# Holding DMA transposes behind weight blocks, a second split of the early v projection, and new orders for five engines

## The chip, the core and the metric

The kernel runs on one core of a Trainium2 chip. Its engines work side by side, each through its own list of instructions in order: TensorE (PE, matmuls, with weight loads shown apart as PEld), ScalarE (ACT), VectorE (DVE), GpSimd (POOL) and SyncE (SP), which here issues nearly all DMAs. They wait for each other by semaphores. The metric is the device time of one execution in microseconds (us).

## What is computed

Two mixers of tokens share one input and are blended by a gate for each row:

```python
x = A_x                                            # 2048 x 448, bf16
g = sigmoid((x * gate_w).sum(-1, keepdims=True))
a = attention(x, wq, wk, wv, wo, beta)             # 16 heads of 28, 4 segments of 512 rows
b = token_mlp(x, w1, b1, w2, b2)
return g * a + (1 - g) * b

# attention, for each segment s and head, phi(t) = t + 1 if t > 0 else exp(t)
p     = softmax(q_s @ k_s.T * 28**-0.5 + causal_mask)
a_mem = (phi(q_s) @ M) / (phi(q_s) @ z + 1e-6)
o     = sigmoid(beta) * a_mem + (1 - sigmoid(beta)) * (p @ v_s)
M, z  = M + phi(k_s).T @ v_s, z + phi(k_s).sum(rows)
# then o @ wo

# token_mlp mixes along the 2048 rows
u = gelu(layernorm(x).T @ w1 + b1)                 # 448 x 1792
y = (u @ w2 + b2).T                                # 2048 x 448
```

## The kernel before

**Pieces and names.** The 2048 rows are 16 tiles of 128, or 4 chunks of 512, one for each segment. The name of an operation is a short word with its numbers:

- `warm`, `fill`: matmuls on constants that keep TensorE running until data arrive. `trx`: TensorE transposes of chunk 0 of x, which `xTcp` copies from PSUM.
- `k0a` to `k0d`, `q0a`, ... and `v03a`, `v67a`, ...: projections (line 705). They use half of the array's rows at a time, two halves side by side, so matmuls come in pairs. `cpk`, `cpq`, `cpv` and `gt` evacuate their PSUM banks (lines 741, 753, 800, 824, 827). `padk`, `padx` and `padq` copy the loaded wk and wq into the padded layout of the heads (line 649).
- `sc4_0` ... are score groups: unit pair 4 (a unit is four heads of one segment, 16 units in all), fill 0 of 5 (line 967). A group fills PSUM banks 0 to 3; `exp4_0` on ScalarE (line 976) empties them, and only then can the next group start. `mask` on GpSimd zeroes what is above the diagonal. `pv` (line 1005) multiplies by v, `mem` reads the memory, `mst` (line 852) adds a segment to it, `wo` is the output projection and `ag` its gated copy (line 1061).
- `ek`, `mk`, `phk`: phi of a key chunk (lines 785, 787, 789), into one of two buffers; `tk1_3` (line 792) is the DMA transpose of chunk 1, head group 3, from this buffer, and frees it. `eq`, `mq`, `phq` are the same for queries.
- `u0-0` to `u13-15` and `y0-0` to `y15-13`: matmuls of the MLP, 14 tiles of u with 16 steps each, 16 tiles of y with 14 steps (line 278; line 280 where one is cut into four matmuls of 32 columns that run side by side). `gsq`, `gvh`, `garg`, `gth`, `gelu` are the gelu (lines 1081, 1084 or 1087, 1089, 1092, 1094); `fin` is the last blend (line 1112). `bns`, `bna`, `ln` are the layernorm (lines 910, 912, 924).
- On SyncE's list: `ldx`, `ldwv`, `ldwk`, `ldwq`, `ldwo` load inputs. `ldw1_0` to `ldw1_6` and `ldw2_0` to `ldw2_7` load blocks of W1 and W2 (lines 570, 576), 1 MB and 0.9 MB, for two tiles of u or of y each. They share three slots, so the fourth block waits until the two tiles of the first are computed. `dtx1_0` ... are DMA transposes of chunks 1 to 3 of x (line 529), each in a piece of three column blocks (_0) and of one (_1). `gk`, `gq` gather the tail dimensions of heads through DRAM (lines 766, 771). `out` stores the result (line 1116).

**What sets the order.** Every engine's sequence is written out by hand in the table `ORDER`, together with the PSUM bank or buffer that an operation takes. `plan` (line 154) reads it, gives every operation its engine (some may go to ScalarE or VectorE) and adds the waits for buffers. An operation's `deps` become semaphore waits ahead of it on its own engine. A waiting instruction holds everything behind it on that engine, and on SyncE that means every later DMA.

**Early v tiles.** `project` (line 698) makes two pairs of outputs from four tiles. For each pair it emits a first part (a or b) and a rest (c or d). With `cut` the first pair's first part is split once more: v03s needs only the first two loaded pieces of WV, v03a all three.

Of the kernel before, what the change touches and what calls it, by code (L numbers as in the profile page):

```python
# [74 lines left out]
class Sched:  # L75
# [78 lines left out]
    def plan(self, order):  # L154
# [22 lines left out]
        self.columns(seq["PE"])  # L177
        assert sum(len(v) for v in seq.values()) == len(self.ops)
# [5 lines left out]
        while moved:  # L184
            moved = False
            for e in ENGINES:
                while head[e] < len(seq[e]):
                    o = seq[e][head[e]]
# [107 lines left out]
def pool_cost(n):  # L296
# [7 lines left out]
        warm fill0 fill1 fill2 fill3 fill4 trx0_1=4 trx0_0=5 trx1_1=6 fill5 gtr trx1_0=7 v03s v03a v03b v03c k0a=45  # L304
        v03d k0c k0b=67 q0a k0d q0b q0d q0c v67a=45 sc0_0 k1a=76 v67c k1c sc0_1 k1b=54 k1d sc0_2 q1a=76 q1b=54 sc0_3
        q1c q1d pv0=7 sc0_4 u0-0:3=6 u1-0=7 btr=5 u2-0=4 u1-1:2 u2-1 u0-3 u1-3 u2-2 u3-0=5 u0-4:2 sc1_0 u0-6 u2-3
        u1-4:2 u0-7 u2-4 u3-1 u0-8 u3-2 u1-6 u3-3 u1-7:3 u2-5 u0-9 u2-6 u3-4 sc1_1 u0-10:2 u1-10:2 u3-5 u0-12 u1-12
        u2-7 u3-6 u1-13 u0-13 u2-8 u0-14:2 u3-7 u1-14:2 u3-8 sc1_2 u2-9:3 pv1=6 u2-12 u3-9:2 u5-0:2=7 u2-13 sc1_3
        u3-11 u2-14 u4-0=6 u5-2 u2-15 u4-1:2 u3-12 u4-3 u5-3 u4-4 u3-13:3 sc1_4 u4-5 u5-4:4 u7-0:2=4 u4-6 u7-2:2 u5-8
        u4-7:2 u7-4 u5-9 sc2_0 u4-9:3 u5-10 u7-5:2 u4-12:3 u6-0=5 u4-15 u5-11:2 u7-7 u6-1:2 sc2_1 u5-13:2 u7-8 u5-15  # L310
        u6-3:3 u7-9 pv2=6 u7-10 sc2_2 u6-6:2 u7-11 mst0=6 u6-8 u7-12 pv3=7 sc2_3 u6-9 u7-13 u6-10 u7-14 u6-11:3 u7-15
        u6-14:2 u9-0=6 u8-0:2=7 sc2_4 u9-1:2 u8-2:2 u9-3 u8-4:2 mem4=4 u8-6:6 u9-4:2 u8-12 sc3_0 u9-6 u8-13 u9-7
        u8-14:2 u9-8:8 pv4=5 sc3_1 k2a=47 k2b=65 k2c k2d sc3_2 q2a=74 q2b=65 q2c q2d sc3_3 v96a=47 v96b=65 v96c v96d
        sc3_4 u10-0:5=7 pv5=5 mem5=6 u10-5:3 pv6=4 sc4_0 mem6=6 u11-0=5 u10-8:2 u13-0=4 u11-1 u13-1 u11-2:3 u12-0=6
        u11-5 u10-10:4 u11-6 u10-14 u11-7 u10-15 sc4_1 u13-2:2 u11-8 u12-1 u11-9:6 u12-2 u13-4 u11-15 u13-5 sc4_2
        u12-3:2 mst1=7 u13-6 u12-5 u13-7 u12-6:2 mem7=7 sc4_3 u12-8:2 u13-8:2 wo3=5 pv7=7 sc4_4 u12-10 u13-10:2
        u12-11:3 wo1=5 u13-12:2 u12-14:2 wo0~2=7 u13-14:2 wo2=5 sc5_0 k3a=76 k3b=54 k3c k3d sc5_1 v14a=76 pv8=5 v14c
        pv9=4 wo5=5 mem9=7 sc5_2 q3a=46 q3b=57 q3c q3d sc5_3 y0-0:2=4 y3-0=6 y0-2 y3-1 y1-0:2=7 y0-3 y1-2 y0-4:2
        y3-2:2 y1-3 mem8=5 y1-4 y0-6 sc5_4 y3-4 y1-5:2 y3-5:3 wo4=5 y1-7 y0-7 sc6_0 y0-8 y1-8 y0-9:3 y3-8:2 y1-9 y3-10
        y1-10:2 sc6_1 y1-12 y3-11:2 y1-13 y0-12 y3-13 y0-13 wo6=5 mem11=7 sc6_2 mst2=6 pv11=5 pv10=7 y4-0:2=4 sc6_3  # L320
        y5-0:2=5 y4-2 y5-2 y2-0:3=7 mem10=6 y2-3:2 y5-3 y4-3 sc6_4 y2-5 y4-4:2 y5-4 y2-6 y4-6 y2-7 y4-7 y2-8 y5-5
        y6-0=6 y5-6 y2-9 sc7_0 y5-7 y6-1 y4-8 y2-10 y5-8 y4-9 y6-2 y4-10 y6-3:2 y4-11:2 sc7_1 y6-5 y4-13 y5-9 y2-11
        y6-6 y5-10 y6-7 y2-12:2 y5-11:3 mem12=4 sc7_2 y6-8:2 pv12=7 wo7=4 y7-0:2=5 sc7_3 y7-2 mem13=7 y7-3 y6-10
        y7-4:5 y6-11 y7-9 wo8=4 y7-10:2 y6-12 y7-12:2 sc7_4 pv14=7 y6-13 pv13=4 wo10=5 wo11=6 wo9=4 pv15=5 y8-0=7
        mem14=6 y8-1:4 y9-0=4 y8-5 y9-1 mem15=6 y9-2 y8-6 y9-3 y8-7 y9-4:2 y8-8 y9-6 y11-0:2=6 y8-9:2 y11-2:2 y9-7
        y11-4 y10-0=5 y9-8 y10-1 y9-9:2 y10-2:2 y8-11:2 y9-11 y11-5 y8-13 y9-12 y11-6 y9-13 y10-4:3 y11-7 y10-7:2
        y11-8 y10-9 y11-9 y10-10:4 y11-10 wo15=7 wo14=4 y11-11 wo12=5 wo13=7 y13-0:2=4 y11-12:2 y13-2 y12-0=5 y14-0=7
        y12-1:2 y14-1:4 y12-3:2 y13-3 y15-0=6 y13-4 y14-5 y15-1 y13-5 y15-2 y12-5 y14-6:2 y15-3 y14-8 y13-6:3 y14-9
        y12-6 y13-9:2 y15-4:2 y14-10 y15-6:2 y13-11 y14-11 y15-8:3 y14-12 y15-11:2 y14-13 y12-7:2 y13-12 y15-13 y13-13
        y12-9:5 y15-0~2=7 y15-1~2 y15-2~2 y15-3~2 y15-4~2 y15-5~2 y15-6~2 y15-7~2 y15-8~2 y15-9~2 y15-10~2 y15-11~2  # L330
        y15-12~2 y15-13~2
    """,
    "ACT": """
        ldx1 ldgwb ldgw xTcp0_01 xTcp0_00 xTcp0_10 cpv0 gt0 cpv2 gt1 gt3 gt2 cpk0_1 ek0_0 cpk0_3 cpq0_3 cpk0_2 cpq0_2
        cpq0_1 gt4 ek0_1 tb exp0_0=2 cpv6 gt7 gt6 exp0_1=3 cpk1_2 exp0_2=4 exp0_3=0 cpq1_1 cpv5 cpq1_2 gt5 exp0_4=1
        eq1_1 exp1_0=5 ek0_2 eq1_2 exp1_1=6 eq1_0 gsq0 gsq1 exp1_2=2 ek0_3 gth0 exp1_3=3 ek1_0 gsq2 gth1 exp1_4=0 gsq3
        ek1_1 gth2 exp2_0=1 gsq4 gth3 exp2_1=4 gsq5 eq1_3 exp2_2=5 gth4 gth5 exp2_3=6 gsq7 gsq6 exp2_4=0 gth7 gth6
        ek1_3 exp3_0=2 gsq8 gsq9 gvh9 ek1_2 exp3_1=3 cpk2_1 cpk2_3 cpq2_3 exp3_2=1 cpq2_1 cpv8 gt8 exp3_3=4 cpv10 gt10
        cpv11 gt12 gt11 gt9 exp3_4=7 ek2_1 eq2_0 exp4_0=0 gth8 gth9 eq2_1 eq2_2 gsq10 exp4_1=5 gvh10 gsq11 exp4_2=6
        gvh11 exp4_3=2 gth10 ek2_0 gth11 exp4_4=3 ag1 gsq12 eq2_3 gsq13 gvh13 exp5_0=1 ek2_3 cpk3_0 cpk3_2 cpk3_3  # L340
        exp5_1=4 cpv14 gt14 cpv15 gt15 ag5 gth12 gth13 exp5_2=7 cpq3_1 cpv13 gt13 exp5_3=0 ek2_2 eq3_1 exp5_4=5 eq3_0
        exp6_0=2 exp6_1=3 ag6 exp6_2=6 eq3_2 exp6_3=0 exp6_4=5 exp7_0=1 exp7_1=4 exp7_2=7 eq3_3 exp7_3=2 ag8 exp7_4=3
        ag10 ag11 ag9 ag15 ag14 ag13
    """,
    "DVE": """
        ob0 bns0 bns3 bna0 bna3 gw bns1 xTcp0_11 bns2 padk1 padx0 padk0 cpv1 padq0 padq3 bna1 padq2 bna2 cpv3 cpk0_0
        ln0 mk0_0 ln2 ln1 phk0_0 bns4 cpv4 bna4 cpq0_0 bns5 bns7 bna5 bns6 bna7 bns8 cpv7 mk0_1 bna6 ln3 bns13 cpk1_0
        cpk1_1 cpk1_3 cpq1_3 bns9 bns12 bns11 bns10 bna10 cpq1_0 bna12 omgh ln6 bna8 bna13 bna11 bna9 ta0 bns15 bns14
        b2c ln4 b1c ln5 ln7 bna14 bna15 ln8 gcol1 ln10 mo0 b1h b1s ln9 oc0 ln12 ln11 gh phk0_1 rec0 mk0_2 ln13 ln14
        mq1_1 ln15 mg0 gcol0 oc1 phk0_2 gvh0 gvh1 garg0 garg1 mq1_2 mo1 oc2 ta1 rec1 mq1_0 mk0_3 oc3 phk0_3 gelu0 mg1  # L350
        gvh2 phq1_0 gelu1 garg2 oa0 gvh3 mo2 garg3 mg2 gelu2 mk1_0 mo3 mk1_1 phk1_1 oa1 gvh4 gelu3 garg4 ta2 gvh5
# [33 lines left out]
def build_kernel(nc, X, WQ, WK, WV, WO, BETA, W1, B1, W2, B2, GW, OUT):  # L385
# [312 lines left out]
    def project(name, outs, prio, cut=False):  # L698
# [21 lines left out]
        for k in range(0, len(outs), 2):  # L720
            a, b = outs[k : k + 2]
            whole = run(a, 0, True), run(b, 1, True)
            if cut and k == 0:
                part(name + "s", [seq[0:2] for seq in whole], (), R_wv[0:2])
                whole = [seq[2:] for seq in whole]
# [519 lines left out]
```

## Time and profile before

| | |
|---|---|
| time, median of 3 | 175.21 us (175.08 to 175.9) |
| profiled execution | 174.94 us, of which the profile's span is 173.2 us |
| granted TensorE clock | full |
| matmuls and weight loads | 1838 and 1846 |
| DMA | 24.55 MB, 142 GB/s over the span |
| start of sc0_0, sc5_0, sc7_4 | 16.46, 98.20, 141.41 us |
| end of the last matmul | 170.79 us |
| landing of a W1 block, min, median, max | 5.8, 6.8, 12.3 us |
| landing of a W2 block | 5.1, 5.5, 8.1 us |
| landing of a tk transpose | 2.4, 2.5, 7.7 us |
| landing of a dtx transpose | 4.1, 5.1, 5.9 us |

A landing is counted from the start of the issue on SyncE. In the page's table of busy time each entry gives the time, the share of the span and the number of instructions. In the rows of 40 slices, a slice is 4.33 us and a digit is its busy share in tenths. In an answer in order of time the columns are start, length, engine, line, operation, tiles, shapes, count, and in brackets the engine's idle time before it with what ended it; "issue" is time for which the profile shows no wait. A TensorE matmul's end is modelled, so the matmul row can look busy through a wait; the weight-load row shows it better.

### The profile page before, as it was taken

To read this page: it belongs to the slowest core of one execution; us is meant where nothing else is said; L and a number is where in the kernel's file an instruction comes from. 1 tells how busy PE (TensorE), PEld (TensorE's weight loads), DVE (VectorE), ACT (ScalarE), POOL (GpSimd) and SP (SyncE) were. 2 spreads that over 40 slices of the span, in tenths; PEclk is the share of its full clock that TensorE was granted. 3 is DMA by queue.
4 is the path that set the end of the run, shared out by engine and by line. 5 is a ranking of instruction groups with operands and counts; after the bars stand their busy time and mean duration, and the time that the engine had idled before them with its cause. 6 is when DMAs were issued, how large, how long until landed. Compare 5 with 4: busy or idle time off the path is not lost.

```text
span 173.2 us, 4524 instructions
## 1 busy us (share of the span) xinstructions
PE 166.6 (96%) x1838; PEld 80.9 (47%) x1846; DVE 144.7 (84%) x323; ACT 128.5 (74%) x154; POOL 69.6 (40%) x99
## 2 busy tenths in 40 slices
PE   8999989999999899999999999999999999999994
PEld 4445334444445345445454445544544445555552
DVE  3769999949999998999989899998997989983115
ACT  2459989799999999999999999987957767004000
POOL 7030097252514620095074472536725955150000
PEclk9999999999999999999999999999999999999999
DMA  5999989248557992097835207211641597408103
GB/s 148 276 183 358 293 143 245 76 89 241 136 139 222 144 169 47 13 271 205 108 67 172 63 0 217 45 30 34 190 113 34 143 300 215 119 22 243 53 0 106
DMA packets 49749, 24.55 MB, mean 142 GB/s; under 512 B 14257, under 2 KB 49489, under 8 KB 49729
## 3 DMA queue, kind: packets, MB, share of 16 engines
q1 hardware_dynamic: 49576, 24.16, 58.0%
q8 instruction: 14, 0.23, 0.6%
q10 hardware_dynamic: 152, 0.12, 0.2%
q14 instruction: 7, 0.05, 0.1%
HBM read 18.76 MB, written 2.36 MB: 122 GB/s over the span
## 4 chain that ended last, share of the span: by engine, by line
PE 60%; DVE 27%; DMA 4%; ACT 3%; issue 2%; SPq 2%; ACTq 0%
PE t L278 35%; PE t L705 13%; PE t L280 5%; PE t L967 4%; PE t L1005 4%; DVE t L1089 3%; DVE t L1094 3%; DVE t L1087 3%; DMA t<-in_A_wk_dram 2%; DVE t L1021 2%; DMA t<-in_A_wo_dram 2%; DVE t L789 2%; DVE t L1040 2%; DVE t L910 1%; ACT t L1081 1%
## 5 line engine op out<-in xcount | busy, mean ns | idle before, releaser
L278 PE MATMUL t<-t 128*128 128x448 bf16 (+2 forms) x441 | 85.8, 347 | 1.1 <-issue 0.8
L976 ACT ACTIVATE t<-t 128x2048 bf16<-128x2048 f32 x40 | 75.0, 1876 | 8.4 <-PE t L967 8.2
L979 POOL TENSOR_SCALAR_AFFINE_SELECT t<-t 128x512 bf16<-128x512 bf16 x64 | 44.4, 717 | 53.7 <-ACT t L976 53.2
L278 PEld LDWEIGHTS t<-t 128*128 128x128 bf16 x449 | 41.5, 98 | 41.2 <-issue 5.9
L705 PE MATMUL t<-t 64*128 64x512 bf16 (+1 forms) x308 | 35.2, 367 | 0.9 <-DMA t<-in_A_wv_dram 0.3
L1036 POOL TENSOR_TENSOR t<-t 128x448 bf16<-128x448 f32 x12 | 15.2, 1274 | 23.6 <-DVE t L1034 13.3
L705 PEld LDWEIGHTS t<-t 64*128 64x128 bf16 x308 | 15.4, 94 | 17.8 <-PE t L705 1.3
L280 PE MATMUL t<-t 128*32 128x448 bf16 (+1 forms) x356 | 20.4, 355 | 0.3 <-DMA t<-in_A_wo_dram 0.3
L1112 DVE SCALAR_TENSOR_TENSOR t<-t 128x448 bf16<-128x448 f32 (+2 forms) x17 | 10.8, 648 | 11.4 <-PE t L278 11.2
L1061 ACT ACTIVATE t<-t 128x448 bf16<-128x448 f32 x10 | 7.2, 724 | 13.8 <-PE t L278 13.5
L967 PE MATMUL t<-t 28*128 28x512 bf16 (+3 forms) x256 | 15.8, 301 | 0.5
L1005 PE MATMUL t<-t 128*32 128x512 bf16 (+3 forms) x256 | 11.4, 300 | 0.5 <-DVE t L893 0.5
L280 PEld LDWEIGHTS t<-t 128*32 128x32 bf16 x356 | 8.4, 96 | 6.8 <-issue 1.8
L967 PEld LDWEIGHTS t<-t 28*128 28x128 bf16 x256 | 4.5, 92 | 14.4 <-ACT t L976 6.2
L1021 DVE STREAM_TRANSPOSE t<-t 128x512 f32<-128x512 f32 x16 | 11.0, 695 | 0.3 <-PE t L1005 0.2
L1042 DVE STREAM_TRANSPOSE t<-t 128x512 bf16<-128x512 bf16 x16 | 11.0, 692 | 0.0
L910 DVE BATCH_NORM_STATS2 t<-t 128x6 f32<-128x448 bf16 x16 | 9.4, 611 | 1.9 <-DMA t<-in_A_x_dram 1.8
L1081 ACT ACTIVATE t<-t 128x448 f32<-128x448 f32 x14 | 8.8, 635 | 1.3 <-DVE t L1094 0.7
L1005 PEld LDWEIGHTS t<-t 128*32 128x32 bf16 x256 | 6.6, 96 | 6.1 <-POOL t L979 1.5
L1089 DVE SCALAR_TENSOR_TENSOR t<-t 128x448 f32<-128x448 f32 x14 | 9.0, 657 | 0.1
L1087 DVE TENSOR_SCALAR t<-t 128x448 f32<-128x448 f32 x10 | 6.5, 667 | 3.1 <-ACT t L1081 3.1
L1019 DVE STREAM_TRANSPOSE t<-t 128x512 f32<-128x512 f32 x12 | 8.4, 700 | 0.7 <-PE t L280 0.3
(73 smaller groups left out, 165.4 us busy)
## 6 DMA issues: line engine op xcount, KB each, us to landing
t<-in_B_w_dram SPq DMA_DIRECT2D x7, 1024.0 KB, 6.8
t<-in_B_w_dram SPq DMA_DIRECT2D x8, 896.0 KB, 5.5
out_dram<-t SPq DMA_DIRECT2D x15, 112.0 KB, 1.8
t<-in_A_x_dram SPq DMA_DIRECT2D x3, 448.0 KB, 5.9
t<-in_A_wo_dram SPq DMA_DIRECT2D x4, 98.0 KB
t<-in_A_wk_dram SPq DMA_DIRECT2D x1, 336.0 KB, 4.0
t<-in_A_wq_dram SPq DMA_DIRECT2D x1, 336.0 KB, 4.6
spare_heads<-t SPq DMA_DIRECT2D x8, 32.0 KB
```

Source lines behind the costliest of these rows:

```text
L278: return e.matmul(out, w, x, skip_group_check=True, **kw)
L280: last = e.matmul(out[q : q + 32], w[:, q : q + 32], x, skip_group_check=True, **kw)
L705: last = e.matmul(bank(o["b"])[:, 0 : o["n"]], o["w"](r, c), o["x"](r, c), start=first, stop=end, skip_group_check=True)
L910: op("DVE", lambda e: e.bn_stats(st6[:, t, :], xh[:, t, :]), reads=[R_x[t]], writes=[R_st6[t]], name=f"bns{t}", cost=512, prio=P_PROJ - 10)
L967: last = e.matmul(bank(hl)[:, c0 : c0 + w], kT[r, hg, s * 512 + j * 128 : s * 512 + j * 128 + 128], qT[r, hg, s * 512 + 128 * j : s * 512 ...
L976: op("ACT", lambda e: e.activation(pslot(g), ps[:, 0:4, :], ACT.Exp, scale=SCALE), reads=R_bank[0:4], writes=[g.res], take=g, name=f"exp{p ...
L979: op("POOL", lambda e, c0=c0: e.affine_select(pslot(g)[:, :, c0 : c0 + 128], pslot(g)[:, :, c0 : c0 + 128], pattern=[[0, 4], [1, 128]], co ...
L1005: last = e.matmul(bank(cb)[32 * hl : 32 * hl + 32, 128 * j : 512], vaug[:, 4 * s + j, 32 * h : 32 * h + 32], pslot(P_fill[u // 2][f])[:, h ...
L1021: dv(lambda e: e.transpose(t2[:, 0, :], bank(cb)[:, 0:512]), [bres(cb)], [R_tt[tb][0]], "ta", 630, use=(cb,))
L1036: op("POOL", lambda e: e.tensor_tensor(o3, n3[0], n3[1], op=ALU.add), reads=R_tt[tb], writes=[R_ob[tb]], name=f"o{u}", cost=1280, port=Tru ...
L1087: alt=("DVE", lambda e: e.tensor_scalar(vh[:, q, :], bank(b)[:, 0:D], 0.5, b1h[:, ft : ft + 1], op0=ALU.mult, op1=ALU.add), dve_cost(448)))
L1089: op("DVE", lambda e: e.scalar_tensor_tensor(gg[:, q, :], gg[:, q, :], 1.0, vh[:, q, :], op0=ALU.add, op1=ALU.mult), reads=[R_gg[q], R_vh[ ...
```

## The change

Three things change together.

1. In `plan`, a DMA transpose of phi of k (`tk`) or of chunk 2 or 3 of x (`dtx2`, `dtx3`) gets one more dependency: the last operation over 1 MB that stands ahead of it on SyncE's list. These are the blocks of W1 and W2 by the sizes that the code notes for them. The transpose, and all that is behind it on the list, is then issued only when that block has landed. The purpose is that a transpose and a weight block ahead of it are not in flight together.
2. `project` with `cut` now splits the second pair's first part too: v03t (first two pieces of WV), then v03b.
3. All five orders are new. The work is the same; its place, its banks, and for some evacuations the engine differ.

The code:

```diff
         self.columns(seq["PE"])
+        big = None
+        for o in seq["SP"]:
+            if big is not None and o.name.startswith(("tk", "dtx2", "dtx3")):
+                o.deps = o.deps + [big]
+            if o.nbytes > 1e6:
+                big = o
...
-            if cut and k == 0:
-                part(name + "s", [seq[0:2] for seq in whole], (), R_wv[0:2])
+            if cut:
+                part(name + "st"[k // 2], [seq[0:2] for seq in whole], (), R_wv[0:2])
                 whole = [seq[2:] for seq in whole]
```

The orders, cut to what the prediction speaks of:

```diff
 "PE":
-        warm fill0 fill1 fill2 fill3 fill4 trx0_1=4 trx0_0=5 trx1_1=6 fill5 gtr trx1_0=7 v03s v03a v03b v03c k0a=45
-        v03d k0c k0b=67 q0a k0d q0b q0d q0c v67a=45 sc0_0 k1a=76 v67c k1c sc0_1 k1b=54 k1d sc0_2 q1a=76 q1b=54 sc0_3
-        q1c q1d pv0=7 sc0_4 u0-0:3=6 u1-0=7 btr=5 u2-0=4 u1-1:2 u2-1 u0-3 u1-3 u2-2 u3-0=5 u0-4:2 sc1_0 u0-6 u2-3
...
-        y1-10:2 sc6_1 y1-12 y3-11:2 y1-13 y0-12 y3-13 y0-13 wo6=5 mem11=7 sc6_2 mst2=6 pv11=5 pv10=7 y4-0:2=4 sc6_3
+        warm fill0 fill1 trx0_1=4 trx0_0=5 trx1_1=6 fill2 fill3 gtr fill4 trx1_0=7 fill5 v03s v03a v03t v03b v03c v03d
+        k0a=54 k0b=67 k0c k0d q0a q0b q0d q0c v67a=54 sc0_0 k1a=67 v67c k1c sc0_1 k1b=45 k1d sc0_2 q1a=76 q1b=45 q1c
+        q1d sc0_3 u1-0:2=7 u0-0:2=6 u1-2 pv0=4 u1-3 u0-2:3 sc0_4 u0-5:2 u1-4 u0-7 btr=4 u3-0=5 u1-5:3 u3-1 u0-8 u3-2
...
+        y3-11:3 y0-13 sc6_2 mem11=6 pv10=5 mst2=4 mem10=7 pv11=6 sc6_3 y5-0=5 y2-0=4 y5-1 y2-1 y5-2:2 y2-2 y5-4:2
+        y4-0=7 y5-6:2 y4-1:3 sc6_4 y4-4 y6-0=6 y5-8 y6-1 y5-9 y4-5 y2-3 y4-6 y2-4 y4-7 y5-10 y6-2 y4-8 sc7_0 y5-11
 "ACT":
-        ldx1 ldgwb ldgw xTcp0_01 xTcp0_00 xTcp0_10 cpv0 gt0 cpv2 gt1 gt3 gt2 cpk0_1 ek0_0 cpk0_3 cpq0_3 cpk0_2 cpq0_2
-        cpq0_1 gt4 ek0_1 tb exp0_0=2 cpv6 gt7 gt6 exp0_1=3 cpk1_2 exp0_2=4 exp0_3=0 cpq1_1 cpv5 cpq1_2 gt5 exp0_4=1
+        ldx1 ldgwb ldgw xTcp0_11 cpv2 gt2 cpv0 cpv1 gt1 gt3 gt0 cpk0_0 ek0_0 cpk0_2 cpk0_3 cpq0_3 cpq0_2 gt4 cpq0_1
+        ek0_1 exp0_0=2 cpv6 gt7 gt6 exp0_1=3 cpk1_3 cpk1_2 exp0_2=4 ek0_2 cpq1_0 cpq1_1 exp0_3=0 cpv5 tb gt5 exp0_4=1
 "SP":
-        ldx0 ldx2 ldwv0 ldwv1 ldwv2 ldwk0 ldwk=0 ldwq0 ldb2 ldbeta ldwq=1 dtx1_0 dtx1_1 ldx4 ldx8 ldx12 ldw1_0 ldw1_1
-        tk0_0 gk0_0 gk0_2 ldb1 ldw1_2 gk0_1 gq0_2 gq0_1 gq0_3 gq0_0 gk0_3 gq0_h1 gq0_h0 gq0_h2 gk0_h1 gk0_h0 tk0_1
-        tk0_2 ldw1_3 tk0_3 ldw1_4 ldw1_5 tk1_1 dtx3_1 dtx2_1 dtx3_0 ldwo1 dtx2_0 tk1_0 gk2_1 ldw1_6 gq2_1 gk2_0 tk1_3
-        gq2_0 ldwo2 ldw2_0 ldwo3 gk2_2 gk2_3 tk1_2 gq2_3 gq2_2 gq2_h2 tk2_1 ldwo0 gk2_h0 gk2_h1 gq2_h0 gq2_h1 ldw2_1
-        gk3_1 ldw2_2 gk3_0 gk3_2 tk2_0 gk3_3 tk2_2 gq3_2 tk2_3 out3 gq3_1 ldw2_3 gk3_h0 gq3_0 out0 gq3_3 gq3_h0 gq3_h1
+        ldx0 ldx2 ldwv0 ldwv1 ldwv2 ldwk0 ldwk=0 ldwq0 ldwq=1 ldbeta ldb2 dtx1_0 dtx1_1 ldx4 ldx12 ldb1 ldx8 dtx2_1
+        tk0_0 ldw1_0 ldw1_1 gk0_2 gk0_1 gk0_3 ldw1_2 gq0_2 gq0_1 gq0_0 gk0_0 gq0_3 gk0_h1 gk0_h0 gq0_h1 gq0_h2 gq0_h0
+        tk0_1 tk0_2 ldw1_3 ldwo2 tk0_3 ldw1_4 dtx2_0 dtx3_0 tk1_1 tk1_0 dtx3_1 ldw1_6 ldw1_5 gk2_1 ldwo1 gq2_3 ldwo3
+        tk1_3 gk2_0 ldwo0 gk2_2 tk1_2 gq2_2 gq2_0 gk2_3 tk2_1 ldw2_1 gq2_1 ldw2_0 gq2_h1 gk2_h1 gq2_h0 ldw2_2 gq2_h2
+        gk2_h0 tk2_0 tk2_3 gk3_0 gq3_3 tk2_2 gq3_0 gq3_2 gq3_1 ldw2_3 gk3_1 out3 gq3_h2 gk3_3 out0 gq3_h0 out1 gk3_2
...
```

## Prediction

> **What bounds the kernel now.** I read the page's busy table first, then its slices, then the waits of TensorE, then its order of time with the stretches between score groups, last the SyncE queue.
>
> ```profile
> PE 166.6 (96%) x1838; PEld 80.9 (47%) x1846; DVE 144.7 (84%) x323; ACT 128.5 (74%) x154; POOL 69.6 (40%) x99
> ...
> PE   8999989999999899999999999999999999999994
> ...
> DVE  3769999949999998999989899998997989983115
> ACT  2459989799999999999999999987957767004000
> ...
> L278 PE MATMUL t<-t 128*128 128x448 bf16 (+2 forms) x441 | 85.8, 347 | 1.1 <-issue 0.8
> L976 ACT ACTIVATE t<-t 128x2048 bf16<-128x2048 f32 x40 | 75.0, 1876 | 8.4 <-PE t L967 8.2
> ```
>
> TensorE is full from end to end; ScalarE and VectorE are full in the slices that hold the attention (about 12 to 120 us) and idle at the tail. So the end is set by TensorE work plus whatever makes TensorE wait, and in the attention ScalarE can be what it waits for: each of the 40 score groups needs the exp of the group before.
>
> A busy PE hides waits, so I turn to rates. From the order of time: 18 plain matmuls of 448 columns take 3.51 us (0.195 each), 14 pairs of key projections 3.13 us (0.224 a pair), 14 pairs of v 2.77 us (0.198), a score group 0.33, a PV unit 0.54 to 0.66 (I take 0.60), an mst 0.5. For ScalarE a full exp is followed 1.78 us after its start by the next instruction; a copy takes 0.5, an exp of 512 or a gelu step 0.53. With these I add up, for each stretch from one score group to the next, the work that the two orders put there. Stretch 0_1 (sc0_1 to sc0_2), for one: a group and seven pairs of k1, 0.33+1.57 = 1.9 on TensorE; exp0_1 and one copy, 1.78+0.52 = 2.3 on ScalarE; measured 2.38, so ScalarE set it.
>
> | stretches | PE work | longer of PE and ACT, stretch by stretch, summed | measured |
> |---|---|---|---|
> | before, sc0_0 to sc5_0 (25) | 77.7 | 81.4 | 81.7 |
> | before, sc5_0 to the last matmul (15) | 72.8 | 73.7 | 72.6 |
>
> The first row holds 4.0 us in which TensorE has no work (81.7-77.7); the second none. Ahead of the first score group, from 6.50 to 16.46 us, the work is 12 pairs of v, 24.5 of k and q, 7.5 more of v: 12x0.198+24.5x0.224+7.5x0.198 = 9.35 us of 9.96, so 0.6 us is lost there. The weight-load row shows by what:
>
> ```profile
> 8.49 1.76 PEld L705 LDWEIGHTS t<-t 64*128 64x128 bf16 x20 [0.55 <-DVE t L649]
> 10.66 2.93 PEld L705 LDWEIGHTS t<-t 64*128 64x128 bf16 x30 [0.41 <-DVE t L649]
> ...
> 16.43 0.13 PEld L967 LDWEIGHTS t<-t 28*128 28x128 bf16 x4 [0.49 <-DVE t L800]
> ```
>
> The padding copies of wk, then of wq (L649) are waited for, then the evacuation of q0 (L800). Two later stalls are on the matmul row itself:
>
> ```profile
> 58.91 0.92 PE L278 MATMUL t<-t 128*128 128x448 bf16 x4 [0.60 <-issue]
> ...
> 91.81 0.94 PE L280 MATMUL t<-t 128*32 128x448 bf16 x16 [0.28 <-DMA t<-in_A_wo_dram]
> ```
>
> [...] the tk transpose issued alone at 43.0 lands after 2.4 us, the one issued at 52.3 behind a weight block of 51.9 lands after 7.0, 0.6 us after that block.
>
> **The change part by part.**
>
> *The waits of tk, dtx2, dtx3.* No byte is moved less. Each waits for the last weight block ahead of it in the queue. In the new queue: tk0_0 and one dtx2 stand ahead of every block and wait for none. tk0_1 waits for w1_2, issued about 24, 7.0 to land as before: 31; the gathers ahead of it end at 34 as now, so nothing. tk0_3 waits for w1_3: issue when u0 and u1 are done, near 37, plus 5.8: 43; behind it stands w1_4, whose slot u3 frees only at 45; the next user of its buffer, the exp of k1_1, now stands behind exp2_0, near 48. dtx2_0 waits for w1_4 (issue 45.5 plus 6.1): 51.6; behind it are dtx3, tk1_1, tk1_0, five issues of 1.2 to 2.2, and landings of 4 to 6 put the last near 65 against 74 for v9-12 and 57 for xT2 against 66. tk1_3 and tk1_2 wait for w1_5, near 70, needed by mst1 near 90; behind them ldwo0, wanted by wo2 at 90. tk2_0 waits for w2_2 (97 plus 5.4), needed near 121; behind it the gathers of k3 and q3, wanted by sc7_2 near 134. Slack is 1 us at tk0_3, 3 at tk0_1 and 8 or more elsewhere: cost 0. Its possible gain: at 58.3 to 58.9 TensorE stands 0.60 us with no wait that the profile shows, while a block, a tk and two dtx are in flight (the DMA share is 1.99 in 56 to 58). Whether that is the cause the trace does not say: 0 to 0.6, I take 0.3.
>
> *The second cut of v03.* v03t needs the first two pieces of WV, but stands behind v03a, which waits for the third. Nothing can start earlier: 0.
>
> *Head of the order.* k0a goes behind v03d: 3 pairs (0.6 us) fill the 0.3 us that TensorE stands before 8.49. ldwq is issued at 4.7, not 5.64, and q0a goes behind k0d, 11 pairs later than now; so the pads of q are long done: 0.2 to 0.4. Three copies of xT go to VectorE, 0.41 each as the one there now; it stands 0.7 and 1.2 us for wk and wq anyhow. Limit of the sum 0.6; I take 0.5, so sc0_0 near 15.9.
>
> *Middle.* By the same rates the new order's longer-of-two sum from sc0_0 to sc5_0 is 81.3 against 81.4. It is 0.9 behind at sc1_0 (stretch 0_2 now has 14 projection pairs, 3.47, and ScalarE an exp and three small jobs, 3.35) but has 1.4 us more matmul work done by then, and has caught up at sc1_1. No gain. The last ldwo, at 88.4, leaves the 0.28 stall at 91.8; it moves to near 75: 0.3, partly inside a stretch that ScalarE sets, so 0.2.
>
> *Tail.* Same work, 72.8 in both, no loss to win. Nearer deadline: y6 starts 6.25 us of TensorE work after y0 ends, whose slot its block w2_3 takes; landing takes 5.5, at most 8.1 for any W2 block. 0 at the median, 0.9 at 7.0. I take 0.
>
> Sum: 0.5+0.3+0.2 = 1.0: 175.2-1.0 = **174.2**.
>
> **Rivals.** *Absorbed.* ScalarE starts exp0_0 only behind 17 copies, tanhs and exps, and VectorE is full: earlier projections then wait for evacuations instead of pads. For: the wait at 16.43 is for a VectorE copy, and the middle's sum is equal. Against: the new order takes one copy off VectorE there. Gain 0.2: **175.0**. *Late blocks, slower.* w1_0 and w1_1 now stand behind tk0_0, which needs phi of k0 (14.5): issue near 15.8 instead of 11.96. With the 9.6 that w1_0 took, it lands at 25.4, while u1-0, moved ahead of sc0_4, wants it at 25.0 (15.9, plus 8.8 for three stretches, plus 0.33): 0.4. If w2_3 takes 7.0, 0.9 more; head gain 0.2. **176.3**. Against: 9.6 was spent behind 1.3 MB of x, which now has a clear road. *All waits fall:* half of the middle's 4.0 us goes: near 172.7; nothing in the sums supports it.
>
> **Numbers.** Forecast 0.50, absorbed 0.29, late blocks 0.18, the last 0.03. The range runs from 173.2, twice the forecast's gain, to 175.9, most of the way to the late blocks. Faster by over 0.5% means under 174.33: most of the forecast's spread and the last, with a little of the absorbed: 0.50; within 0.5%: 0.32; slower 0.18.
>
> **What would show it.** Right: no wait for L649 on the weight loads of 8 to 11 us, first score group near 15.9; no stall of 0.6 by "issue" near 58; tk landings of 2.4 to 3; sc5_0 at 97.2 or so instead of 98.20. Wrong: an L278 wait for B_w near 25 or 126, SyncE waits after which a gather or a block lands late, or a first score group that is no earlier.

## The result, and the profile after

The changed kernel takes **174.22 us** (median of four runs, 174.12 to 174.29), the kernel before 175.48 beside it (175.08 to 175.9): ratio 0.9928, interval 0.9899 to 0.9956. Run again among the experiments, it took 174.69 against 175.02, ratio 0.9963, interval 0.9945 to 0.998 (22 and 59 runs). So by the medians it is faster by 1.26 us in the first comparison and by 0.33 in the second; by the ratios, by 1.3 and 0.65. The second rests on many more executions. 174.2 was forecast, 1.0 us less than 175.2.

Single executions of one kernel spread by some 0.7 us either way (22 runs of the kernel after lie between 173.77 and 175.23). A profile is one execution, so its stalls are compared stretch by stretch. A median here is that of all executions, while a ratio and its interval leave out the slow ones (over 1.5% above the fastest of their kernel), so a ratio need not be the quotient of two medians.

The page of the kernel after, the rows that answer to those shown of before: busy times, slices, the largest group of matmuls and the group of those that are cut into four.

```profile
PE 167.8 (97%) x1900; PEld 81.5 (47%) x1900; DVE 146.2 (85%) x326; ACT 126.3 (73%) x151; POOL 68.3 (40%) x99
...
PE   7999999999999999999999999999999999999994
...
DVE  0889999879898999998989999998999699885123
ACT  2178998799998999999999989997747876003000
...
L284 PE MATMUL t<-t 128*128 128x448 bf16 (+2 forms) x431 | 83.0, 347 | 0.0
...
L286 PE MATMUL t<-t 128*32 128x448 bf16 (+1 forms) x428 | 24.7, 356 | 0.3 <-DVE t L1027 0.2
```

Nothing in the busy times tells of a faster kernel: TensorE's row is 1.2 us longer, in a span that is 0.7 shorter (172.5 against 173.2). Line numbers are 6 higher after `plan`: L284 is the L278 of before, and its idle time went from 1.1 to 0.0. The work of the two orders is not quite the same: `columns` cuts a matmul into four by what stands beside it, and in the new order 18 more are cut (428 records on this line instead of 356). That is most of the rise from 1838 to 1900 matmul records.

Where the time went is seen with the prediction's rates: for each stretch between two score groups, the measured length less TensorE's work at those rates is what was *lost* in it. The last column is an experiment of below, the kernel before with one edit on SyncE's list: the DMA transposes of x (dtx) ahead of a weight block.

| us | before | after | after, run again | before, dtx first |
|---|---|---|---|---|
| first score group (sc0_0) | 16.46 | 16.33 | 16.71 | 16.68 |
| lost in 0_1, 0_2, 0_3 | 1.57 | 1.40 | 0.76 | 1.56 |
| lost in 1_3 and 2_1 | 0.52 | 0.02 | 0.03 | 0.51 |
| lost in 1_4 | 0.01 | 0.12 | 1.25 | 0.02 |
| lost in 2_2 | 0.20 | 0.45 | 0.54 | 0.20 |
| lost in 2_3 | 0.78 | 0.03 | 0.02 | 0.03 |
| lost in 3_1 | -0.01 | 0.29 | 0.29 | 0.26 |
| lost in 4_3 | 0.47 | 0.04 | 0.04 | 0.01 |
| all from sc0_0 to sc5_0 | 4.00 | 2.94 | 3.53 | 3.05 |
| lost in 5_1 and 6_2 | 0.29 | 0.87 | 0.88 | 0.30 |
| all from sc5_0 on | -0.17 | 0.38 | 0.37 | -0.18 |
| end of the last matmul | 170.79 | 170.15 | 171.11 | 170.05 |

Before to after: 0.13 gained ahead of sc0_0, 1.06 in the middle, 0.55 given back behind sc5_0; together 0.64. The 0.13 cannot be told from chance: sc0_0 starts at 16.46 to 16.71 in the five profiles with the old head, and at 16.33 to 17.02 in the five in which the new head is unchanged. The head first, on the weight-load row: in the kernel before, the matmul row shows no gap from 7.27 to 16.38, where the weight loads wait 0.55 and 0.41. Weight loads of the kernel after in order of time:

```profile
6.57 2.93 PEld L711 LDWEIGHTS t<-t 64*128 64x128 bf16 x32 [0.17 <-DMA t<-in_A_wv_dram]
9.79 3.60 PEld L711 LDWEIGHTS t<-t 64*128 64x128 bf16 x36 [0.28 <-DVE t L655]
13.94 1.79 PEld L711 LDWEIGHTS t<-t 64*128 64x128 bf16 x20 [0.56 <-PE t L711]
16.30 0.13 PEld L973 LDWEIGHTS t<-t 28*128 28x128 bf16 x4 [0.56 <-ACT t L808]
```

The wait for the padding copies fell from 0.55 plus 0.41 to 0.28, but the last row, the score group's wait for the evacuation of q0, grew from 0.49 to 0.56. At the two places of the middle that the prediction named, matmuls of the kernel after, with no idle time in brackets any more:

```profile
55.73 0.39 PE L973 MATMUL t<-t 28*128 28x512 bf16 x4
56.06 2.82 PE L284 MATMUL t<-t 128*128 128x448 bf16 x14
58.82 0.40 PE L973 MATMUL t<-t 28*128 28x384 bf16 x8
...
90.06 0.39 PE L973 MATMUL t<-t 28*128 28x512 bf16 x4
90.38 2.28 PE L284 MATMUL t<-t 128*128 128x448 bf16 x11
92.60 0.40 PE L973 MATMUL t<-t 28*128 28x384 bf16 x8
```

And what the new waits of the transposes cost SyncE (line, what it waited for, total, times, longest):

```profile
SPq L276 <- DMA t<-in_B_w_dram: 7.1, 2, 3.8
...
SPq L535 <- DMA t<-in_B_w_dram: 5.4, 1, 5.4
```

L276 waits for semaphores where an operation has more than one. The second row is dtx2_0, which stands until w1_4 has landed at 51.31. The first is tk0_3, from 40.1 until w1_3 has landed at 43.42 (it is issued at 43.49), and tk2_0, held from 97.9 to the landing of w2_2 at 101.67; tk2_0 is issued only at 106.77, so another wait ends later there. No other wait of the rule shows: the blocks of the others had landed when SyncE came to them. What the rule holds in earnest is dtx2_0: in the kernel without it (below) tk0_3 still went out at 44.42, 0.1 us before its block had landed, but dtx2_0 at 47.02, 5.5 us before w1_4 had landed (52.51).

### The profile page after: what moved, and what is told of

It is laid out like the page before. It is cut to its first block, busy times and chain, and to the rows that moved or that the text cites. A ratio compares the mean times of both kernels' runs of the same rounds, so it can differ in the third digit from the quotient of the medians.

```text
span 172.5 us, 4631 instructions
## 1 busy us (share of the span) xinstructions
PE 167.8 (97%) x1900; PEld 81.5 (47%) x1900; DVE 146.2 (85%) x326; ACT 126.3 (73%) x151; POOL 68.3 (40%) x99
## 4 chain that ended last, share of the span: by engine, by line
PE 75%; DVE 13%; SPq 6%; DMA 4%; issue 1%
PE t L284 44%; PE t L286 12%; PE t L711 7%; PE t L973 6%; PE t L1011 5%; DMA t<-in_A_x_dram 4%; SPq L535 2%; DVE t L916 2%; DVE t L749 1%; SPq L524 1%; PE t L858 1%; DVE t L1048 1%; DVE t L930 1%; DVE t L761 1%; DVE t L1071 1%
## 5 line engine op out<-in xcount | busy, mean ns | idle before, releaser
L284 PE MATMUL t<-t 128*128 128x448 bf16 (+2 forms) x431 | 83.0, 347 | 0.0
L985 POOL TENSOR_SCALAR_AFFINE_SELECT t<-t 128x512 bf16<-128x512 bf16 x64 | 42.5, 684 | 47.1 <-ACT t L982 46.6
L284 PEld LDWEIGHTS t<-t 128*128 128x128 bf16 x431 | 39.6, 98 | 38.6 <-issue 4.6
L286 PE MATMUL t<-t 128*32 128x448 bf16 (+1 forms) x428 | 24.7, 356 | 0.3 <-DVE t L1027 0.2
L1067 ACT ACTIVATE t<-t 128x448 bf16<-128x448 f32 x11 | 7.8, 722 | 14.5 <-PE t L284 14.4
L286 PEld LDWEIGHTS t<-t 128*32 128x32 bf16 x428 | 10.3, 96 | 8.6 <-issue 2.2
L1011 PE MATMUL t<-t 128*32 128x256 bf16 (+3 forms) x256 | 11.9, 300 | 0.2 <-DVE t L918 0.2
L1011 PEld LDWEIGHTS t<-t 128*32 128x32 bf16 x256 | 6.7, 96 | 5.8 <-issue 2.0
L1100 DVE SCALAR_TENSOR_TENSOR t<-t 128x448 bf16<-128x448 f32 x14 | 9.0, 646 | 0.4 <-ACT t L1098 0.4
```

Of the source, the lines that this page charges most:

```text
L284: return e.matmul(out, w, x, skip_group_check=True, **kw)
L286: last = e.matmul(out[q : q + 32], w[:, q : q + 32], x, skip_group_check=True, **kw)
L985: op("POOL", lambda e, c0=c0: e.affine_select(pslot(g)[:, :, c0 : c0 + 128], pslot(g)[:, :, c0 : c0 + 128], pattern=[[0, 4], [1, 128]], co ...
L1011: last = e.matmul(bank(cb)[32 * hl : 32 * hl + 32, 128 * j : 512], vaug[:, 4 * s + j, 32 * h : 32 * h + 32], pslot(P_fill[u // 2][f])[:, h ...
```

## The experiments

Twelve kernels ran, in three groups, each with its own runs of the kernel before. Their medians were 175.02, 175.03 and 174.70, so ratios are compared, not times.

### What are the waits and the cut worth in the new order?

The kernel after once more, without the rule in `plan`, and with v03t merged back into v03b:

```diff
 # waits out
-        big = None
-        for o in seq["SP"]:
...
 # second cut out
-            if cut:
-                part(name + "st"[k // 2], ...
+            if cut and k == 0:
+                part(name + "s", ...
```

> The changed kernel once more, as the measure for the others of this group. Every theory expects 174.2 us, 0.993 of the kernel before.

> The changed kernel without the new waits of tk, dtx2 and dtx3; orders and cuts stay. Theory 1 (the gain is the orders' own, the waits are free): within 0.3 us of the changed kernel, first score group at 16.3 us, no new stall of TensorE over 0.3 us. Theory 2 ([...] the 0.60 us stall by issue at 58.3 us of the kernel before): transposes of chunk 2 and 3 are issued at 46 us right behind w1_4 and tk1_1 near 52; a stall of 0.3 to 0.7 us by issue comes up between 46 and 65 us, time 174.5 to 174.9.

> The changed kernel with v03t and v03b in one part, as before. Prediction's step (no use in the second cut, since v03t stands behind v03a): within 0.1 us of the changed kernel. Rival (v03t starts ahead of something that v03b waits for): sc0_0 later by 0.2 to 0.4 us.

Measured: 174.69, ratio 0.9963 (0.9945 to 0.998), for the kernel after; 174.82, 0.997 (0.9948 to 0.9992), without the waits; 174.53, 0.9968 (0.9948 to 0.9988), without the second cut. The three intervals lie on each other. In the new order the rule and the cut neither cost nor bring anything that 22 executions of each can show, and 2_3 loses 0.02 to 0.03 in all three: the stall of 58.3 stays away without the rule, as theory 1 had it. Their first score groups start at 16.71, 17.02 and 16.76, within the spread of the head.

The profiled execution of the kernel after shows a stall that the first one has not, on the matmul row:

```profile
43.43 1.31 PE L284 MATMUL t<-t 128*128 128x448 bf16 x6
45.79 1.50 PE L284 MATMUL t<-t 128*128 128x448 bf16 x7 [1.05 <-DMA t<-in_B_w_dram]
```

This is u7-0, moved ahead by the change, waiting for w1_3. The block took 7.8 us from its issue here (37.98 to 45.74) and 6.1 in the first execution (37.31 to 43.42, with u7-0 near 45.0). So the new order had a margin of about 1.6 us at this block in the first execution. Nine profiles with the new order are on record; this is the only one that used it up (in the eight others the block took 5.9 to 7.2 us).

### What do the waits do in the old order?

```diff
 # the kernel before
         self.columns(seq["PE"])
+        big = None
+        for o in seq["SP"]:
+            if big is not None and o.name.startswith(("tk", "dtx2", "dtx3")):
+                o.deps = o.deps + [big]
+            if o.nbytes > 1e6:
+                big = o
```

> The kernel before with the new waits alone; orders and cuts stay. Theory 1 (the waits only pay with the new orders): tk1_1 is held until w1_5 lands at 58.7, the dtx behind it go out between 60 and 66, chunk 2 lands near 70 and k2a, wanted at 67.2, makes TensorE wait about 3 us: 177 to 179 us. Theory 2 (traffic in flight together causes the stall of 0.60 us at 58.3): that stall is gone whatever the total. Rival (the waits bring the gain by themselves): 174.2 to 174.9.

Measured: 184.31, ratio 1.0488 (1.0435 to 1.0541). The direction was expected, the size was not: one stall had been counted on, there are several. Stretch 3_1 alone loses 4.40 us; the matmuls there, in order of time:

```profile
68.11 0.40 PE L973 MATMUL t<-t 28*128 28x384 bf16 x8
71.17 4.24 PE L711 MATMUL t<-t 64*128 64x512 bf16 x22 [2.66 <-DMA t<-in_A_x_dram]
```

k2a waits for the transposes of chunk 2 of x (dtx2). They stand behind tk1_1, which now waits for w1_5 (landing 60.88), and the last of them lands at 71.12 instead of 65.80: one waiting transpose holds all that is behind it on SyncE's list. Further 1.44 us go in 0_4, where the load of b1 stands behind the waiting tk0_0, and 2.14 in 4_3, where TensorE waits for wo. Yet 2_3 loses only 0.03: with no transpose beside w1_5 (53.93 to 60.88; tk1_1 is issued at 60.95), the stall of 58.3 is gone.

### Is it the place of the transposes of x?

In the new list the dtx stand ahead of the block w1_5. (The expectations also call the dtx gathers; they are not the gk and gq.) The kernel before with this one edit:

```diff
-ldw1_4 ldw1_5 tk1_1 dtx3_1 dtx2_1 dtx3_0 ldwo1 dtx2_0 tk1_0
+ldw1_4 dtx3_1 dtx2_1 dtx3_0 dtx2_0 ldw1_5 tk1_1 ldwo1 tk1_0
```

> The kernel before with one edit on SyncE's list: the four dtx of chunks 2 and 3 go ahead of w1_5 (right behind w1_4) and tk1_1 behind it, so that only one tk and no dtx is in flight with w1_5 at 53 to 58 us. Theory 2 (traffic in flight together causes the 0.60 us stall by issue at 58.3): the stall is under 0.2 us, sc2_4 comes 0.5 us earlier, and 0.2 to 0.6 us of it are left at the end: 174.7 to 175.2 where the kernel before has 175.3. Rival (the stall has another cause[...]): it stays at 0.5 to 0.7, same time.

Measured: 174.15, ratio 0.9952 (0.9932 to 0.9971). Its matmuls between 56 and 60 us:

```profile
56.33 0.40 PE L967 MATMUL t<-t 28*128 28x512 bf16 x4
56.66 2.63 PE L278 MATMUL t<-t 128*128 128x448 bf16 x13
59.22 0.40 PE L967 MATMUL t<-t 28*128 28x384 bf16 x8
```

The score group behind comes 2.89 us after the one ahead, 3.65 in the kernel before. All else in the table is as before, but for the 0.46 that came back in 4_3 and 0.27 that went in 3_1. The rival, a stall that stays, fell; the gain is larger than expected, as 4_3 was not in the sum. One edit of one list thus gives what the whole change gives, as far as the intervals tell.

Then the same list with the order of the small transfers changed behind the block, and, the other way round, the new order with w1_5 put back ahead of the dtx (and the rule taken out, as SyncE would else stand):

```diff
 # the kernel before, tk1_1 behind the dtx
-ldw1_4 ldw1_5 tk1_1 dtx3_1 dtx2_1 dtx3_0 ldwo1 dtx2_0 tk1_0
+ldw1_4 ldw1_5 dtx3_1 dtx2_1 dtx3_0 dtx2_0 tk1_1 ldwo1 tk1_0
 # the kernel after without the rule, w1_5 early
-ldw1_4 dtx2_0 dtx3_0 tk1_1 tk1_0 dtx3_1 ldw1_6 ldw1_5
+ldw1_4 ldw1_5 dtx2_0 dtx3_0 tk1_1 tk1_0 dtx3_1 ldw1_6
```

> The kernel before with the transpose tk1_1 and the four gathers dtx in the other order on SyncE's list, all of them behind the block ldw1_5 as before: ldw1_5 dtx3_1 dtx2_1 dtx3_0 dtx2_0 tk1_1. Theory T (the stall of 58.3 comes from a block and transposing transfers in flight together, whichever they are[...]): the stall stays, stretch 2_3 loses 0.5 to 0.8[...], ratio 0.998 to 1.000. Rival K (it comes from the tk transpose issued right behind the block): 2_3 loses 0.03 as with all of them ahead of the block, ratio 0.995. Rival P[...]: some other loss between.

> The kernel after without its rule of waits and with the block ldw1_5 put back where the kernel before has it, behind ldw1_4 and ahead of dtx2_0, dtx3_0, tk1_1: it is issued near 51.9, when u5 is done, and two gathers and a transpose stand behind it. Theory T[...]: a stall without a wait comes back, 0.3 to 0.8 us lost in 2_3 or 2_4, ratio to before 0.999. Rival P[...]: 2_3 and 2_4 lose under 0.1, ratio 0.996.

Measured: 176.57 (five executions only), ratio 1.0087 (1.0054 to 1.0121), and 174.92, ratio 1.0018 (0.9999 to 1.0036). In the first, 2_3 loses 0.45: the stall stays, against K, but is smaller than T had it, as P allowed. A new one is larger. Its matmul row:

```profile
58.82 0.92 PE L278 MATMUL t<-t 128*128 128x448 bf16 x4 [0.27 <-issue]
...
68.44 0.82 PE L705 MATMUL t<-t 64*128 64x512 bf16 x6 [0.93 <-DVE t L1087]
```

And ScalarE's row tells where the second comes from:

```profile
62.25 1.04 ACT L1092 ACTIVATE t<-t 128x448 f32<-128x448 f32 x2 [0.25 <-DVE t L1089]
64.65 0.63 ACT L785 ACTIVATE t<-t 128x512 bf16<-128x512 bf16 x1 [1.36 <-DMA t<-t]
65.19 1.86 ACT L976 ACTIVATE t<-t 128x2048 bf16<-128x2048 f32 x1
66.95 1.15 ACT L1081 ACTIVATE t<-t 128x448 f32<-128x448 f32 x2
```

tk1_1, last in the queue, lands at 64.63; the exp ek1_3 that takes its buffer over waits 1.36 us for it, the exp of a score group stands behind ek1_3, and the gelu step gsq8 behind that. gvh8 (line 1087) follows gsq8 and is the last to read the PSUM bank of tile u8; k2a takes this bank, and TensorE waits for it until 68.44. A transpose that nobody needs soon still holds a buffer.

In the second, no stall came back near 58: 2_3 and 2_4 lose 0.03 and 0.02, though a block and two dtx were in flight together (w1_5 issued at 51.50, landing at 57.63; dtx2_0 issued at 51.93, dtx3_0 at 56.77). Theory T, that a block beside transposes makes the stall wherever it falls, is wrong. It also follows that the place of w1_5 alone does not keep the stall away in the new order; which part of the order does is open. But this order gives up 0.005 against the kernel after without the waits (ratios 1.0018 and 0.997, measured in different groups): 3_1 loses 0.79, with a wait of 0.35 at 68.11 for the same line 1087 as in the kernel above.

### The wo block

```diff
-gq2_0 ldwo2 ldw2_0 ldwo3 gk2_2 ... tk2_1 ldwo0 gk2_h0
+gq2_0 ldwo2 ldw2_0 ldwo3 ldwo0 gk2_2 ... tk2_1 gk2_h0
```

> The kernel before with the last load of wo moved from 88.4 to about 80 us on SyncE's list. Prediction's step: the wait of 0.28 us at 91.8 goes; ScalarE needs 0.74 us more than TensorE in that stretch (3.23 against 2.49), so sc4_4 can come 0 to 0.2 us earlier: within 0.2 us of the kernel before. If it is a full gain: 0.4 us.

Measured: 174.82, ratio 0.9995 (0.9977 to 1.0013), nothing. The stall of 91.8 went (4_3 lost 0.01), and in the profiled execution a new one came further on:

```profile
126.03 2.06 PE L278 MATMUL t<-t 128*128 128x448 bf16 x10
128.30 0.74 PE L278 MATMUL t<-t 128*128 128x448 bf16 x3 [0.20 <-DMA t<-in_B_w_dram]
```

w2_3 was 0.44 us earlier on its way, took 6.9 us instead of 5.5, and y6 met it: 0.41 lost in 6_4. A gain ahead of a transfer with a tight deadline is lost again when that transfer is slow. One execution shows this; how often it happens does not show.

### The head

Two edits of the kernel after: the transposes of x behind the fill matmuls as before; and the evacuations of q0 ahead of the layernorm statistics on VectorE and ahead of gt4 on ScalarE.

```diff
 # fill
-warm fill0 fill1 trx0_1=4 trx0_0=5 trx1_1=6 fill2 fill3 gtr fill4 trx1_0=7 fill5 v03s
+warm fill0 fill1 fill2 fill3 fill4 trx0_1=4 trx0_0=5 trx1_1=6 fill5 gtr trx1_0=7 v03s
 # evacuations
-phk0_0 ln1 bns4 cpv4 bna4 cpq0_0 bns5          -cpq0_2 gt4 cpq0_1
+phk0_0 ln1 cpv4 cpq0_0 bns4 bna4 bns5          +cpq0_2 cpq0_1 gt4
```

> The changed kernel with the constant matmuls (warm, fill) and transposes at the start in the order of the kernel before. Theory (v03s starts at 6.29 instead of 5.87 because transposes, gtr and fills are interleaved so that trx1_0 and fill5 end late): v03s at 5.9 us, v03a at 6.5 as the data set it; sc0_0 is gated by evacuations, so it moves by less than 0.15 us, time within 0.2 us of the changed kernel. Rival (the start is what cost the head its gain): sc0_0 at 15.9 to 16.0, 0.3 us gained.

> The changed kernel with the evacuations ahead of the first score group put first: on VectorE cpv4 and cpq0_0 ahead of bns4 and bna4, on ScalarE cpq0_1 ahead of gt4. Theory (sc0_0 waits for cpq0_0 on VectorE and cpq0_1 on ScalarE, 16.18 us both, not for projections that end near 15.7): sc0_0 at 15.7 to 15.9 and exp0_0 at 16.2 to 16.4, 0.3 to 0.6 us gained there; at the end 0.1 to 0.5 us. Rival (bns4 later holds the layernorm, and the gain is lost at u0 and u1): sc0_0 earlier, sc1_1 unchanged at 34.1, same time.

Measured: 174.39, ratio 0.9965 (0.995 to 0.998), with sc0_0 at 16.22; and 174.83, 0.9997 (0.9979 to 1.0014), with sc0_0 at 16.30. The ratio of the first is that of the kernel after (0.9963 in another group). Still, the two kernels with this edit, this one and the last of the experiments, have the earliest sc0_0 of all profiles, 16.22 and 16.03; whether that is a gain is not settled. The theory behind the second fell. ScalarE's row, then VectorE's, of that kernel:

```profile
14.81 1.24 ACT L808 ACTIVATE t<-t 128x512 bf16<-128x512 f32 x2 [0.36 <-PE t L711]
...
14.81 0.62 DVE L832 CAST t<-t 128x448 bf16<-128x448 f32 x1 [0.28 <-PE t L711]
15.46 0.69 DVE L806 CAST t<-t 128x512 bf16<-128x512 f32 x1
```

With nothing ahead of them, both engines stand until 14.81, when the last q0 part has ended, and then need 1.24 to 1.34 us for two evacuations each (the banks of one v pair and of q0 are those that the score group fills). 14.81+1.34 = 16.15, and the group starts at 16.30: the evacuations bound the head, not their place in the lists.

The profile of the other kernel shows a wait that the change brought in, on VectorE, just behind the start of the score groups:

```profile
18.23 0.63 DVE L916 BATCH_NORM_STATS2 t<-t 128x6 f32<-128x448 bf16 x1 [0.50 <-DMA t<-in_A_x_dram]
```

The statistics bns8 wait for ldx8, which the new list has as the last load of x, behind ldx12 and ldb1. It lands at 17.2 to 19.1 us in the kernels with the new list; in the five with the old one, at 15.2 to 16.7. VectorE has no time to spare there (busy 7.93 of the 8 us from 18 to 26 in the kernel after), so the copies of k1 and q1 behind it are late. The executions with the new lists of VectorE and ScalarE fall in two sorts by it:

| kernel | ldx8 lands | VectorE waits for it | lost in 0_1 to 0_3 |
|---|---|---|---|
| after, run again | 17.45 | 0 | 0.76 |
| eq2_3 earlier (below) | 17.78 | 0 | 0.76 |
| w1_5 early, waits out | 17.91 | 0 | 0.76 |
| after | 17.99 | 0.17 | 1.40 |
| fill | 18.21 | 0.50 | 1.73 |
| second cut out | 18.73 | 0.48 | 1.73 |
| waits out | 19.08 | 0.57 | 1.80 |

The kernel before lost 1.57 in these three stretches. So the new order is better there by 0.8 us where ldx8 lands in time, and between 0.2 better and 0.2 worse where it is late. Seven executions show the two going together; to load x8 earlier alone was not tried.

### What was given back behind sc5_0

> The kernel after with eq2_3 ahead of exp5_1 on ScalarE, nothing else. Theory: in stretch 5_1 ScalarE has 4.54 us of work beside 3.92 of TensorE, since eq2_3 (0.5) was put there; ahead of exp5_1 it stands in stretch 5_0, where TensorE has 3.4 and ScalarE less than that; the loss of 5_1 falls from 0.67 to about 0.15 and all later starts come 0.4 to 0.5 earlier; ratio 0.994. Rival: eq2_3 then waits for its multiplication on VectorE and holds exp5_1 by 0.3 or more: no gain, ratio 0.996 to 0.998.

> The kernel after with three edits of order: the warm-up matmuls and the transposes of x as in the kernel before; eq2_3 moved from behind the gelu steps gt15, gt14 to ahead of exp5_1 on ScalarE; cpq1_3 moved ahead of bns9 on VectorE. Theory of single stalls (each loss of the ledger is a stall of its own, and taking it away moves the end): stretch 5_1 from 0.67 lost to about 0.15, stretch 0_2 from 0.37 to about 0.1, first score group at 16.2; the last matmul near 169.4 against 170.15, median 173.8, ratio to before near 0.993 where the kernel after had 0.996. Rival (given back): the stretch 0_2 is not set by the copy of q1 but by the exps, which follow one another without a gap until stretch 1_0; then its 0.37 turns up in 0_3, and the total is 0.4 better at most; ratio 0.995.

```diff
-exp5_0=1 cpk3_0 cpk3_3 exp5_1=4 cpv15 gth13 gt15 gt14 eq2_3 ag5
+exp5_0=1 cpk3_0 cpk3_3 eq2_3 exp5_1=4 cpv15 gth13 gt15 gt14 ag5
 # the second has also the edit "fill" and, on VectorE
-cpk1_0 bns9 cpq1_3 bna11
+cpk1_0 cpq1_3 bns9 bna11
```

Measured: 174.58, ratio 1.0002 (0.9979 to 1.0025); and 175.21, ratio 1.0029 (1.0011 to 1.0048). Both fail. In the first, 5_1 loses 0.96 instead of 0.67. ScalarE's row:

```profile
101.04 0.63 ACT L815 ACTIVATE t<-t 128x512 bf16<-128x512 bf16 x1 [0.44 <-DMA t<-spare_heads]
```

eq2_3 reads what a gather through DRAM brings, and that is not there yet: 0.44 us of waiting, and exp5_1 stands behind it. The rival was right in kind, though it named VectorE's multiplication instead of the gather. But exp5_1 ends at 103.44 and the next score group starts only at 104.78, so this exp is not what TensorE waits for. Its weight loads between the two show what is:

```profile
103.40 0.50 PEld L286 LDWEIGHTS t<-t 128*32 128x32 bf16 x16 [0.47 <-DVE t L1027]
104.45 0.10 PEld L286 LDWEIGHTS t<-t 128*32 128x32 bf16 x4 [0.55 <-ACT t L833]
```

The first wait, of wo5 for VectorE's copy of pv8, is in the kernel after too, and just as long (see the tail, below); moving eq2_3 did not touch it. The second is new: mem9 takes a bank of the v pair that gt (line 833) still reads, and gt15 and gt14 stand behind exp5_1. So the theory aimed at a wait that did not set the stretch.

In the second kernel, bringing the copy of q1 ahead took 0.20 off 0_2 against the kernel after (0.10 against the executions in which ldx8 landed in time), and its matmul row shows where it went:

```profile
24.98 1.14 PE L286 MATMUL t<-t 128*32 128x448 bf16 x20
27.07 0.73 PE L1011 MATMUL t<-t 128*32 128x512 bf16 x16 [0.95 <-DVE t L918]
```

pv0 takes the bank of the last copy of q1. With the statistics that now come later ahead of it, that copy runs from 26.24 to 26.93, no earlier than in the kernel after (26.05 to 26.74), though the score group 0_3 starts 0.68 earlier; so pv0 waits, and 0_3 loses 1.23. Together 0_1 to 0_3 lose 1.88, though ldx8 landed early here, at 17.24. That copy is L806; the row names L918, a short instruction that ends just behind it. The rival "given back" held, and more than all was given back. No version ran that beats both kernels clearly: the dtx ahead of w1_5 in the old order (0.9952) and the whole change (0.9963 in another group) overlap in their intervals.

## Why the prediction was right, and where not

**What bounds the kernel.** Right: TensorE's work from sc0_0 to sc5_0 is the same in both orders at the prediction's rates (81.74-4.00 = 80.68-2.94 = 77.7 us), and what moved is the time between.

**The waits of tk, dtx2, dtx3, cost 0.** Right in the new order: with and without them 0.9963 and 0.997. The reason given, slack behind each waiting instruction, is what the old order lacks, where the same rule costs 0.0488. The tightest place named, "1 us at tk0_3", showed no stall of TensorE. The tk transposes behind w1_3 on the list land after 2.4 to 3.6 us in the kernel after, except tk2_1 with 4.3; tk1_1 took 2.6 instead of 7.0.

**Gain at the stall of 58.3, taken as 0.3 in 0 to 0.6.** The term was too small: 2_3 went from 0.78 lost to 0.03, 0.75 us. And it was put under the waits; it comes from the order. The kernel before gains it with the dtx ahead of the block and no rule, and the kernel after keeps it without the rule.

**The second cut, 0.** Right: 0.9968 against 0.9963.

**The head, 0.5.** This step failed: 0.13, which is within the spread of sc0_0 from one execution to another. The pads were hidden as worked out (0.96 us of waits became 0.28), but the evacuations of q0 took their place. The rival "absorbed" had said so and was set behind for its reason against, that VectorE has one copy less there: two evacuations each on two engines bind even with nothing ahead of them. The step treated the waits for pads as the only ones and left the 0.49 of the old profile, for the copy of q0, out of the sum.

**The middle, no gain by equal sums.** Failed in its reading, not in its sums. "Longer of two" of 81.3 against 81.4 cannot see single stalls: 1_3 and 2_1 lost 0.50 less and 0_1 to 0_3 0.17 less, while 2_2 and 3_1 lost 0.55 more. In the profile these nearly cancel, so the zero held by cancellation. The stall for the last ldwo was taken as 0.2; stretch 4_3 lost 0.43 less. But 4_3 also lost nothing in the old order with the dtx first, where ldwo0 keeps its place and was issued at 87.55 instead of 88.39, and moving ldwo0 alone moves no median.

**The tail, 0.** Failed: 0.55 given back. The deadline named, w2_3 at y6, was kept (landing 125.19). The larger part is in 5_1, which lost 0.24 before and 0.67 after, and there TensorE waits for VectorE. Weight loads of the kernel after from pv9 to sc5_2, then the matmuls of the kernel before at the same place:

```profile
102.99 0.50 PEld L1011 LDWEIGHTS t<-t 128*32 128x32 bf16 x16 [0.37 <-issue]
103.96 0.69 PEld L286 LDWEIGHTS t<-t 128*32 128x32 bf16 x20 [0.47 <-DVE t L1027]
105.05 0.12 PEld L973 LDWEIGHTS t<-t 28*128 28x128 bf16 x8 [0.40 <-issue]
...
104.23 0.73 PE L1005 MATMUL t<-t 128*32 128x512 bf16 x16
104.78 1.15 PE L280 MATMUL t<-t 128*32 128x448 bf16 x20
105.86 0.40 PE L967 MATMUL t<-t 28*128 28x256 bf16 x8
```

In both orders wo5 takes the PSUM bank of pv8, which VectorE's transposing copy ta8 (line 1027, 1021 before) has to empty. In the kernel after, ta8 runs from 103.19 to 103.91 and starts 0.8 us behind the end of pv8's matmuls (102.39), for the evacuation cpk3_2, which ScalarE did before, and mk2_0 now stand ahead of it on VectorE's list. In the kernel before it started 0.2 us behind pv8, at 103.80, and wo5 followed without a wait. The experiments with eq2_3 took ScalarE's work for the cause (4.54 us in this stretch beside 3.92 of TensorE); but exp5_1 ends at 102.93, 2.1 us ahead of sc5_2. No run moved ta8. The prediction summed PE work alone behind sc5_0, because the old order had lost nothing there, and it did not ask which bank a moved evacuation keeps from TensorE.

**Late blocks.** w1_0 landed at 22.81, ahead of u1-0 near 25.6, since it took 7.4 us and not the 9.6 taken over from before. A late block did occur, at w1_3 and u7-0, 1.05 us in one of nine profiles with the new order; it was not among the deadlines named.

**The sum.** Forecast 0.5+0.3+0.2 = 1.0. By the same steps the two profiles give 0.13 in the head, 0.75 at 58.3, 0.43 in 4_3, -0.12 in the rest of the middle, -0.55 in the tail: 0.64 in this pair of executions. 1.26 is the difference of the first medians, 0.33 that of the repetition. By the ratio of the repetition the gain is 0.65, two thirds of the forecast. That the first median met 174.2 so closely is luck: the terms were off by errors of both signs, and the first comparison had four executions of each kernel.

**What stays open.** Why the stall of 58.3 exists. Edits on SyncE's list alone take it away (2_3 loses 0.03 with the dtx first and with the rule alone), while in the new order a block and two dtx in flight together did not bring it (0.03 in 2_3, 0.02 in 2_4 with w1_5 early). What TensorE waits for in it no trace names ("issue", 0.60 us in the kernel before); that other transfers in flight cause it was the author's guess and is not shown. Nor is it shown why 2_2 loses 0.02 to 0.70 among the new orders, partly as 0.30 us of "issue".

## What to carry to other kernels

Ask of a new order not only whether the sums of work per stretch allow it, but which buffers, banks and loads its moved instructions wait for: here gains were given back at waits that nobody had listed (q0's evacuations, x8, w1_3, a bank that VectorE empties later). When a large change moves the time by half a per cent, try its single edits on the old kernel: moving four transfers ahead of one block did as much as five new orders, within the intervals. Before an experiment is built on a sum of work, look up which wait ends last in that stretch: eq2_3 was moved for a wait that was VectorE's. And a rule that adds waits to a shared queue was free in the order made for it; in the old one it cost 5%.

## What was not expected of the hardware

- The landing of one and the same 1 MB block, issued within 0.7 us of the same moment, took 6.1 us in one execution and 7.8 in another; a 448 KB load (ldx8) took 5.5 to 6.8 in the nine profiles with the new list. A margin of 1.6 us behind the usual landing was missed in one of the nine.
- TensorE stood for 0.27 to 0.61 us with nothing that the trace names, at the same score group in three kernels (before, wo block moved, tk1_1 behind the dtx), and did not in two others with the same order on TensorE that differ from them on SyncE alone (dtx first, rule alone).
